# Routing among experts: a planner that counts VectorE's low parts from when they can begin, flag tiles cleared first, single tiles counted in round 0

## Chip, cores and metric

One core of a Trainium2 chip runs the kernel. The metric is the device time of one execution in microseconds (us), lower is better. The profiler's span (first to last instruction of the program) is a little shorter than the device time.

## What is computed

Attention over 4 x 8 heads of 768 tokens (a window of 31 keys around each query, and 24 block summaries), whose output of 3072 tokens x 512 goes into a mixture of 8 experts. The routing is greedy over all token-expert pairs in the order of their logits, with 384 places per expert:

```python
logits = x @ w_gate                       # 3072 x 8
for idx in np.argsort(-logits.flatten()):
    tok, e = idx // E, idx % E
    if assigned[tok] >= 0 or counts[e] >= cap:   # cap = 3072 // 8 = 384
        continue
    assigned[tok] = e; counts[e] += 1
for e in range(E):
    mask = assigned == e
    out[mask] = np.maximum(x[mask] @ w1[e], 0.0) @ w2[e]    # 512 -> 1024 -> 512
```

## The kernel before, in words

**Three parts follow each other.** Attention, ordered by a list scheduler of its own (`plan`), ends with the logits of 24 tiles of 128 tokens. Routing round 0 then finds the first expert that fills up, and its 384 tokens. Then eight experts run one after the other, in the order in which they fill; here they are called expert 0 to expert 7. Round r+1 of the routing runs beside expert r or earlier ones, piece by piece.

**An expert** has two stages on TensorE. The h stage is 96 matmuls of 128x384 (8 blocks f of 12, L786), the y stage 72 matmuls of 128x512 (24 groups of 3, L803). All products are made of a high and a low part: ScalarE copies a high part (`ah`, `bh` of the weights, `xh` of the tokens, `hh` of the hidden values), VectorE subtracts it and so leaves the low part (`al`, `bl` L620, `xl` L654, `hl` L793). The tokens of the next expert are gathered from DRAM (`xg`, GpSimd's queue) and transposed on TensorE into PSUM banks, 3 transposes for each of 4 slices of the model dimension; one such group of 3 is called a flip here (`flip_x`). The 4 PSUM banks of the flips are those in which the next h stage accumulates.

**A round of routing** is a serial chain between TensorE and VectorE. `aim` marks each token's best expert with places left. `search` then finds a rank threshold in 3 digits, and is done twice: for a digit, `compare` writes 0/1 tiles for 24 token tiles (VectorE, in two halves, `g`), 12 small matmuls count them per expert (L471, called a count here), VectorE turns the counts into flags (`full`, L475 to L477), a single matmul reduces the flags (L480, called a step), and VectorE sets the next thresholds (`piv`, L484). In a count one matmul takes two token tiles at once: tile t against its own experts and tile t+1 against its own, with 16 columns, of which two blocks are used and added. After the second search two prefix matmuls (L548, L549) and 12 matmuls (L580) give the 384 token indices; `close` and the next `aim` follow.

**The planner** is a clock in Python, not on the chip: `state["now"]` advances by a cost for each matmul that is written out (0.174 for the h stage, 0.228 for the y stage), and `state["dve"]` says until when VectorE has work. `service` writes out low parts that are due, and `advance` the next piece of the routing as soon as its wait has passed on that clock. So costs and waits in `TUNE` decide between which expert matmuls a routing matmul stands, and TensorE, ScalarE and VectorE each then work in the order written. `prepare` places the flips of the next expert in the y stage: from group 9 on if the round is finished and the tokens were fetched `xw` before, at intervals of `fp`; whatever is left stands behind the last y matmul.

```python
def vector(cost):                                        # L694
    state["dve"] = max(state["dve"], state["now"] + TUNE["hop"]) + TUNE["dv"] * cost
```

Round 0 is not among experts: nothing else is left for TensorE, and its steps follow each other as fast as they can. GpSimd has work of its own before the first flags: `count`, `place` and `slot` (L455 to L460), which use SBUF space that attention held until its last output tiles are in DRAM, and then the clearing of the two flag tiles `full0`, `full1` (L464).

## Time and profile before

| | before |
|---|---|
| device time, 3 runs | 488.83, 490.3, 491.13 us (median 490.3) |
| profiled execution | 490.43 us, of it span 488.7 us |
| attention | 0 to 135 us of the span |
| round 0 up to the first expert matmul | 135 to 164 us |
| eight experts | 164.3 to 479.3 us |
| last rows to DRAM | to 488.7 us |
| TensorE busy | 449.5 us (92%) |
| VectorE busy | 348.8 us (71%) |
| ScalarE, GpSimd busy | 212.7 us, 129.8 us |

The busy time of an engine is a mean over stages with different limits. A matmul's row shows when it starts and how long until its result is there; matmuls of one kind start closer to each other than their rows are long. "idle before" in square brackets is the time in which the engine had nothing to do before a row, and what released it.

### The profile page before, as it was taken

The page shows a single profiled execution, that of the slowest core. Times are in us where ns is not written, and L with a number is a line of the kernel's source. Part 1 is how long each engine was busy: PE and PEld are TensorE (multiplying, and loading weights), DVE is VectorE, ACT ScalarE, POOL GpSimd, SP SyncE. Part 2 cuts the span into 40 slices and gives each one's busy share as a digit, 9 for nine tenths or more (in the row PEclk, how much of TensorE's full clock was granted, in tenths as well). Part 3 has the DMA queues.
Part 4 walks back from the last instruction along what each step waited for, and adds up shares of the span by engine and source line. Part 5 has one row for each costly group of instructions (what it writes and reads, how often), then busy time and mean ns, then how long its engine had stood idle before and what let it go on. Part 6 is the DMA issues. An engine that isn't in the chain of part 4 may idle for free.

```text
span 488.7 us, 12165 instructions
## 1 busy us (share of the span) xinstructions
PE 449.5 (92%) x4655; PEld 374.2 (77%) x4655; DVE 348.8 (71%) x1349; ACT 212.7 (44%) x449; POOL 129.8 (27%) x211
## 2 busy tenths in 40 slices
PE   7999999999925899999989989999998998999992
PEld 6686877878814797698778779769877876989981
DVE  5989888869758888867777777786778756561510
ACT  3796877858401442441353154144125306443400
POOL 2596939234111101400320230040023025002010
PEclk9999999999955999999999999999999998999997
DMA  8998392211203803800930660380083069621001
GB/s 307 410 313 314 92 393 89 74 46 67 89 1 108 302 2 131 317 28 18 331 126 1 229 245 1 108 336 32 4 317 154 1 218 345 235 87 65 1 23 43
DMA packets 22426, 73.32 MB, mean 150 GB/s; under 512 B 3168, under 2 KB 3424, under 8 KB 21984
## 3 DMA queue, kind: packets, MB, share of 16 engines
q1 hardware_dynamic: 16608, 53.67, 30.6%
q0 software_dynamic: 5760, 18.88, 10.3%
q8 instruction: 37, 0.61, 0.5%
q14 instruction: 21, 0.17, 0.1%
HBM read 59.95 MB, written 12.58 MB: 148 GB/s over the span
## 4 chain that ended last, share of the span: by engine, by line
PE 70%; issue 13%; DVE 10%; DMA 3%; POOL 2%; ACT 1%; POOLq 0%; SPq 0%; DVEq 0%
PE h L786 21%; PE y L803 20%; PE o L366 6%; PE s L330 5%; PE t L134 5%; DVE al L620 4%; PE x L134 3%; PE l L372 3%; PE r L471 3%; DVE g L106 1%; POOL out L769 1%; DVE xl L654 1%; PE x L272 1%; PE y L739 1%; DMA xd<-x 1%
## 5 line engine op out<-in xcount | busy, mean ns | idle before, releaser
L803 PE MATMUL y<-bl,hh 128*128 128x512 f32 x192 | 76.9, 401 | 0.0
L803 PE MATMUL y<-bh,hl 128*128 128x512 f32 x192 | 76.8, 400 | 0.0
L803 PE MATMUL y<-bh,hh 128*128 128x512 f32 x192 | 76.5, 399 | 0.0
L631 POOL DMA_INDIRECT xg<-xd,idx x24 | 23.2, 968 | 188.4 <-issue 136.8
L617 ACT ACTIVATE ah<-raw 128x1024 fp32r<-128x1024 f32 (+1 forms) x36 | 34.0, 965 | 83.6 <-DMA raw<-w1r 65.6
L786 PE MATMUL h<-xh,ah 128*128 128x384 f32 x256 | 60.4, 350 | 8.1 <-DVE xl L654 3.6
L790 ACT ACTIVATE hh<-h 128x384 fp32r<-128x384 f32 x64 | 31.5, 491 | 83.0 <-PE h L786 70.0
L786 PE MATMUL h<-xl,ah 128*128 128x384 f32 x256 | 61.1, 347 | 0.7
L793 DVE SCALAR_TENSOR_TENSOR hl<-h,hh 128x384 fp32r<-128x384 f32 x64 | 35.4, 553 | 35.2 <-ACT hh L790 32.6
L345 ACT ACTIVATE pe<-sm,mx 128x120 f32<-128x120 f32 x192 | 57.8, 385 | 0.3
L786 PE MATMUL h<-xh,al 128*128 128x384 f32 x256 | 56.4, 341 | 0.0
L769 POOL DMA_INDIRECT out<-y,idx x24 | 29.6, 1233 | 98.8 <-ACT y L767 92.4
L786 PEld LDWEIGHTS h<-xh,ah 128*128 128x128 f32 x256 | 45.2, 191 | 12.6 <-ACT xh L651 5.7
L786 PEld LDWEIGHTS h<-xl,ah 128*128 128x128 f32 x256 | 45.4, 189 | 3.7 <-DVE xl L654 3.7
L786 PEld LDWEIGHTS h<-xh,al 128*128 128x128 f32 x256 | 45.6, 190 | 0.0
L338 DVE CUSTOM_DVE_ANT_0 sm<-s,cs 128x120 f32<-128x120 f32 x192 | 41.2, 277 | 5.5 <-PE s L330 4.9
L803 PEld LDWEIGHTS y<-bh,hh 128*128 128x128 f32 x192 | 36.1, 188 | 6.5
L803 PEld LDWEIGHTS y<-bh,hl 128*128 128x128 f32 x192 | 36.2, 189 | 6.2
L803 PEld LDWEIGHTS y<-bl,hh 128*128 128x128 f32 x192 | 36.2, 188 | 6.1
L620 DVE TENSOR_TENSOR al<-raw,ah 128x1024 fp32r<-128x1024 f32 (+1 forms) x36 | 38.9, 1097 | 0.6 <-ACT ah L617 0.6
L620 DVE TENSOR_TENSOR bl<-raw,bh 128x1024 fp32r<-128x1024 f32 x32 | 38.9, 1215 | 0.0
L617 ACT ACTIVATE bh<-raw 128x1024 fp32r<-128x1024 f32 x32 | 33.7, 1053 | 1.0 <-DMA raw<-w2r 1.0
(139 smaller groups left out, 738.1 us busy)
## 6 DMA issues: line engine op xcount, KB each, us to landing
raw<-w1r SPq DMA_DIRECT2D x32, 512.0 KB
raw<-w2r SPq DMA_DIRECT2D x32, 512.0 KB, 4.2
kd<-kT SPq DMA_DIRECT2D x16, 400.0 KB, 5.5
vw<-v SPq DMA_DIRECT2D x24, 260.0 KB, 10.1
xd<-x POOLq DMA_DIRECT2D x24, 256.0 KB
qt<-qT SPq DMA_DIRECT2D x3, 1536.0 KB
qt<-qT SPq DMA_DIRECT2D x3, 512.0 KB
xg<-xd,idx POOLq DMA_INDIRECT x24
```

The source lines that it names most:

```text
L134: nc.tensor.transpose(o, i, idn)
L330: nc.tensor.matmul(PS[2 * t + k][x * 64:x * 64 + 64, p], QT[b % 2][r, (i + x) // FIRST, p, (i + x) % FIRST], keys(b, p, r, i + x), start=T ...
L338: nc.vector.tensor_tensor_reduce(sm[:, p], PS[u][:, p], m, -0.125, 3e38, op0=OP.add, op1=OP.min, accum_out=mx[:, p:p + 1])
L345: nc.scalar.activation(PE_[u][:, p], SM[u][0][:, p], AF.Exp, bias=SM[u][1][:, p:p + 1], scale=-1.0)
L366: nc.tensor.matmul(po(t, s)[x * 64:x * 64 + 64, p], PT[u][:, p, x * 64:x * 64 + 64], VW[b % 2][:C, i - s + x, 2 * p + s], start=True, stop ...
L617: nc.scalar.activation(hi[:, c], raw[:, c], AF.Copy)
L620: nc.vector.tensor_tensor(lo[:, c], raw[:, c], hi[:, c].bitcast(F32), op=OP.subtract)
L769: st = nc.gpsimd.indirect_dma_start(out=out, out_offset=bass.IndirectOffsetOnAxis(ap=ROUND[r][1][:, c:c + 1], axis=0), in_=y, in_offset=None)
L786: nc.tensor.matmul(ph, a[:, d], b[:, d], start=n == 0, stop=n == 11)
L790: nc.scalar.activation(hh[:, f], ph, AF.Relu)
L793: nc.vector.scalar_tensor_tensor(hl[:, f], ph, 0.0, hh[:, f].bitcast(F32), op0=OP.max, op1=OP.subtract)
L803: nc.tensor.matmul(py[c], a[:, f, s], b, start=f == 0 and i == 0, stop=f == 7 and i == 2)
```

## The change

Four things. The planner's `vector` takes a time since which the work can begin, and low parts pass the time at which their high part was written out plus `lb` (0.75) or `wb` (1.25), instead of the time at which they themselves are written out. The waits of the routing pieces have other numbers and a second part that occupies VectorE without delaying the next matmul; a flip costs 0.57 on the planner's clock instead of 0.33, a count 0.36 instead of 0.41. The two flag tiles are cleared near the program's start. In round 0 a count takes single token tiles: 24 matmuls of 8 columns, and one instruction on VectorE makes the flags and their maximum. Rounds 1 to 7 keep pairs.

```diff
-    y2=0.45, y2m=0.021, y3=1.7,
+    y2=0.55, y2m=0.0064, y2r=0.23, y3=1.25, y3r=0.5, lb=0.75, wb=1.25, fx=0.57,
...
+    fulls = [rt.tile([128, E + 1], BF, name=f"full{k}") for k in range(2)]
+    for full in fulls:
+        nc.gpsimd.memset(full, 0.0)
+
     first = targets(0)
...
-    fulls = [rt.tile([128, E + 1], BF, name=f"full{k}") for k in range(2)]
-    for full in fulls:
-        nc.gpsimd.memset(full, 0.0)
-
-    def search(R, oh, dup, g, digits):
+    def search(R, oh, dup, g, digits, pairs):
         for i, n in enumerate(digits):
-            pc = R[:, 384:384 + 2 * E]
-            for t in range(0, NT, 2):
-                nc.tensor.matmul(pc, g[t // HT][:, t % HT * n:t % HT * n + 128], oh[:, t:t + 2].rearrange("p t e -> p (t e)"), start=t == 0, stop=t == NT - 2)
+            m = 2 if pairs else 1
+            pc = R[:, 384:384 + m * E]
+            for t in range(0, NT, m):
+                nc.tensor.matmul(pc, g[t // HT][:, t % HT * n:t % HT * n + 128], oh[:, t:t + m].rearrange("p t e -> p (t e)"), start=t == 0, stop=t == NT - m)
...
-            nc.vector.tensor_scalar(short[:n], pc[n:2 * n, E:], -1.0, CAP - 0.5, op0=OP.mult, op1=OP.add)
-            nc.vector.tensor_tensor(full[:n, :E], pc[:n, :E], short[:n], op=OP.is_ge)
-            nc.vector.tensor_reduce(full[:n, E:], full[:n, :E], axis=AX.X, op=OP.max)
-            yield 0.017 * NT, TUNE["y1"]
+            if pairs:
+                short = rt.tile([64, E], F32, name="short", bufs=2)
+                nc.vector.tensor_scalar(short[:n], pc[n:2 * n, E:], -1.0, CAP - 0.5, op0=OP.mult, op1=OP.add)
+                nc.vector.tensor_tensor(full[:n, :E], pc[:n, :E], short[:n], op=OP.is_ge)
+                nc.vector.tensor_reduce(full[:n, E:], full[:n, :E], axis=AX.X, op=OP.max)
+            else:
+                nc.vector.tensor_scalar(full[:, :E], pc, CAP - 0.5, 0.0, op0=OP.is_ge, op1=OP.max, accum_out=full[:, E:])
+            yield 0.36, TUNE["y1"]
...
-                yield 0.03, TUNE["y2"] + m * TUNE["y2m"]
+                yield 0.05, TUNE["y2"] + n * TUNE["y2m"], TUNE["y2r"] + n * TUNE["y2m"]
...
-            yield 0.03, TUNE["y3"]
+            yield 0.05, TUNE["y3"], TUNE["y3r"]
...
-            def low(c=c):
+            def low(c=c, since=state["now"] + TUNE["wb"]):
                 nc.vector.tensor_tensor(lo[:, c], raw[:, c], hi[:, c].bitcast(F32), op=OP.subtract)
-                vector(0.06 + 1.08 / n)
+                vector(0.06 + 1.08 / n, since)
...
-    def vector(cost):
-        state["dve"] = max(state["dve"], state["now"] + TUNE["hop"]) + TUNE["dv"] * cost
+    def vector(cost, since=None):
+        state["dve"] = max(state["dve"], state["now"] + TUNE["hop"] if since is None else since) + TUNE["dv"] * cost
...
-            state["now"] += 0.33
+            state["now"] += TUNE["fx"]
```

What this does to the order is seen in three places. Up to the end of attention all engines keep their order, but for two clears on GpSimd.

The first place is GpSimd's queue ahead of round 0. Before:

```order
L455 TENSOR_SCALAR count<-colsi 128x128 x3
L457 CAST place<-cb 128x2
L459 TENSOR_TENSOR slot<-cb 128x3
L460 TENSOR_SCALAR slot<-slot 128x3
L464 MEMSET full_2940 128x9
L464 MEMSET full_2941 128x9
```

And of the change, GpSimd's first rows in the program, ahead of all work that waits for a transfer:

```order
L96 MEMSET g_77 128x832
L96 MEMSET g_78 128x832
L96 MEMSET g_79 128x832
L96 MEMSET g_80 128x832
L138 MEMSET full_85 128x9
L138 MEMSET full_86 128x9
```

The clears no longer stand behind `count`.

The second place is TensorE at the end of expert 2's y stage, where expert 3's tokens are flipped (`h<-cs,xg`), a step stands (`r<-full,steps`) and expert 3's first matmuls follow. Before:

```order
L134 MATMUL h<-cs,xg 128x128 x3
L803 MATMUL y<-bl,hh 128x512
L480 LDWEIGHTS steps
L480 MATMUL r<-full_2941,steps 128x9
L803 MATMUL y<-bh,hl 128x512
L803 MATMUL y<-bh,hh 128x512
L803 MATMUL y<-bl,hh 128x512
L803 MATMUL y<-bh,hl 128x512
L803 MATMUL y<-bh,hh 128x512
L134 MATMUL h<-cs,xg 128x128 x9
L786 MATMUL h<-xh,ah 128x384 x4
```

Of the change, the end of the same stage, with the first matmuls of a count behind the last y matmul:

```order
L807 MATMUL y<-bl,hh 128x512
L484 LDWEIGHTS steps
L484 MATMUL r<-full_86,steps 128x9
L807 MATMUL y<-bh,hl 128x512
L807 MATMUL y<-bh,hh 128x512
L807 MATMUL y<-bl,hh 128x512
L807 MATMUL y<-bh,hl 128x512
L807 MATMUL y<-bh,hh 128x512
L472 LDWEIGHTS g_77
L472 MATMUL r<-oh,g_77 128x16
```

No flip is left there; the four stand behind y matmuls 30, 39, 48 and 57 of the 72. Expert by expert, the y matmuls behind which the next expert's four flips stand are: before 66, 72, 72, 72 in experts 0 to 4, then 63, 69, 72, 72 in expert 5 and 27, 39, 51, 63 in expert 6; of the change 60, 66, 72, 72 in expert 0, then 54, 66, 69, 72 in expert 1, then 30, 39, 48, 57 in experts 2 to 4, and 27, 36, 45, 54 in experts 5 and 6. The rounds run ahead: the routing's last matmul before stands behind y matmul 66 of expert 5, and of the change behind h matmul 29 of that expert.

The third place is VectorE at the same end of expert 2's y stage. Before, up to expert 3's first count:

```order
L106 TENSOR_TENSOR g_78<-dup,piv 128x768
L488 TENSOR_SCALAR below<-piv 128x1
L620 TENSOR_TENSOR al<-raw,ah 128x1024
L654 TENSOR_TENSOR xl<-h,xh 128x384
L620 TENSOR_TENSOR al<-raw,ah 128x1024
L654 TENSOR_TENSOR xl<-h,xh 128x384
L620 TENSOR_TENSOR al<-raw,ah 128x1024
L654 TENSOR_TENSOR xl<-h,xh 128x384 x2
L475 TENSOR_SCALAR short<-r 64x8
```

Of the change, from the last `xl` of that stage on:

```order
L658 TENSOR_TENSOR xl<-h,xh 128x384
L477 TENSOR_SCALAR short<-r 32x8
L478 TENSOR_TENSOR full_86<-r,short 32x8
L479 TENSOR_REDUCE full_86<-full_86 32x1
L488 TENSOR_SCALAR piv<-cs,r 128x32
L106 TENSOR_TENSOR g_77<-dup,piv 128x384
L106 TENSOR_TENSOR g_78<-dup,piv 128x384
L492 TENSOR_SCALAR below<-piv 128x1
L477 TENSOR_SCALAR short<-r 32x8
```

The three `al` and four `xl` that stood last have moved forward in the stage, and search steps stand at its end.

## Rows read from the trace of the kernel before

**Rows 1.** The page's first lines: the span, and TensorE's busy time, share of the span and instructions.

```profile
span 488.7 us, 12165 instructions
...
PE 449.5 (92%) x4655; PEld 374.2 (77%) x4655; DVE 348.8 (71%) x1349; ACT 212.7 (44%) x449; POOL 129.8 (27%) x211
```

**Rows 2.** Busy time of each engine by stage, cut at the first matmul of each h and y stage: h and y of expert 0, 1, 4, 5 and 6, and h of expert 7. Behind the colon of a stretch stands its length, then the engines as the first line names them.

```profile
core 0: us, PE busy (x) PEld busy (x) DVE busy (x) ACT busy (x) POOL busy (x), PEclk, DMA share, GB/s
...
164.30:183.35 19.05, 19.05 (x149) 17.79 (x150) 16.28 (x44) 9.42 (x15) 0.00 (x0) 1.00 0.33 129
183.35:204.54 21.19, 20.30 (x139) 15.49 (x138) 16.71 (x65) 5.94 (x9) 4.94 (x8) 1.00 0.59 210
204.54:224.27 19.73, 19.41 (x136) 17.44 (x136) 14.95 (x36) 8.90 (x15) 2.09 (x3) 1.00 0.18 70
224.27:245.48 21.21, 20.30 (x138) 15.46 (x137) 16.46 (x64) 5.99 (x9) 5.00 (x8) 1.00 0.62 223
...
327.41:347.19 19.78, 19.45 (x135) 17.48 (x136) 14.95 (x36) 8.85 (x15) 2.15 (x3) 1.00 0.15 59
347.19:368.36 21.17, 20.28 (x139) 15.47 (x138) 16.47 (x64) 5.99 (x9) 5.02 (x8) 1.00 0.60 213
368.36:388.10 19.74, 19.40 (x136) 17.44 (x137) 14.96 (x36) 8.85 (x15) 2.16 (x3) 1.00 0.17 66
388.10:408.27 20.17, 19.66 (x120) 14.97 (x120) 13.85 (x57) 4.55 (x8) 3.97 (x6) 1.00 0.60 214
408.27:428.70 20.43, 18.80 (x99) 18.11 (x98) 11.29 (x16) 10.28 (x16) 6.90 (x10) 0.92 0.74 270
428.70:446.53 17.83, 17.83 (x86) 14.65 (x85) 8.55 (x10) 7.33 (x11) 0.29 (x1) 1.00 0.15 54
446.53:463.19 16.66, 16.66 (x97) 16.66 (x96) 7.30 (x10) 7.96 (x13) 2.93 (x6) 1.00 0.13 48
```

**Rows 3.** The timeline where round 0's first flags are made: start, length, engine, line, operation.

```profile
135.64 0.17 DVE L475 TENSOR_SCALAR short<-r 64x8 f32<-64x8 f32 x1 [0.33 <-PE r L471]
135.88 1.54 POOL L455 TENSOR_SCALAR count<-colsi 128x128 f16<-128x128 int16 x3 [3.98 <-DMA xd<-x]
...
137.96 0.15 POOL L464 MEMSET full<- 128x9 bf16 x2
138.10 0.16 DVE L476 TENSOR_TENSOR full<-r,short 64x8 bf16<-64x8 f32 x1 [2.30 <-POOL full L464]
...
138.51 0.19 PE L480 MATMUL r<-full,steps 128*128 128x9 bf16 x1 [2.98 <-DVE full L477]
```

**Rows 4.** Later steps of round 0 in the timeline, and, as the last line, a group of the list by line: the accumulator reads that follow attention's masked minimum (shapes, count, busy us and mean ns).

```profile
140.06 0.16 DVE L475 TENSOR_SCALAR short<-r 32x8 f32<-32x8 f32 x1 [0.36 <-PE r L471]
140.33 0.15 DVE L476 TENSOR_TENSOR full<-r,short 32x8 bf16<-32x8 f32 x1
140.51 0.15 DVE L477 TENSOR_REDUCE full<-full 32x1 bf16<-32x8 bf16 x1
...
140.72 0.19 PE L480 MATMUL r<-full,steps 128*128 128x9 bf16 x1 [0.70 <-DVE full L477]
...
144.73 0.47 PE L471 MATMUL r<-oh,g 128*128 128x16 bf16 x12 [1.64 <-DVE wh L516]
...
L338 DVE DVE_READ_ACCUMULATOR2_ANT mx<- 128x1 f32 x192 | 15.9, 83 | 0.0
```

**Rows 5.** The timeline where expert 2 hands over to expert 3.

```profile
282.55 0.49 PE L134 MATMUL h<-cs,xg 128*128 128x128 f32 x3
...
284.41 1.15 PE L134 MATMUL h<-cs,xg 128*128 128x128 f32 x9
...
286.31 1.21 DVE L620 TENSOR_TENSOR al<-raw,ah 128x1024 fp32r<-128x1024 f32 x1
286.45 0.62 PE L786 MATMUL h<-xh,ah 128*128 128x384 f32 x2 [0.89 <-DVE xl L654]
```

**Rows 6.** The timeline of a count and of a step among y matmuls of expert 2.

```profile
281.01 0.46 PE L471 MATMUL r<-oh,g 128*128 128x16 bf16 x12
281.33 0.47 PE L803 MATMUL y<-bh,hl 128*128 128x512 f32 x1
281.64 0.39 PE L803 MATMUL y<-bh,hh 128*128 128x512 f32 x1
...
283.12 0.18 PE L480 MATMUL r<-full,steps 128*128 128x9 bf16 x1
283.15 0.48 PE L803 MATMUL y<-bh,hl 128*128 128x512 f32 x1
```

**Rows 7.** The end of a round among experts, from the prefix matmul on, in the timeline; then two groups of the page, with shapes, count, busy us and mean ns.

```profile
271.37 0.18 PE L548 MATMUL r<-inc,cb 128*128 128x2 bf16 x1
...
271.61 0.41 DVE L555 SCALAR_TENSOR_TENSOR place<-inc,r,ge 128x24 f16<-128x24 bf16 x2 [0.63 <-PE r L549]
...
273.84 0.16 DVE L581 COPY hit<-r 128x3 f32<-128x3 f32 x1
...
277.73 0.36 DVE L127 TENSOR_TENSOR oh<-cand,tgt 128x192 bf16<-128x192 bf16 x1
...
L793 DVE SCALAR_TENSOR_TENSOR hl<-h,hh 128x384 fp32r<-128x384 f32 x64 | 35.4, 553 | 35.2 <-ACT hh L790 32.6
L620 DVE TENSOR_TENSOR bl<-raw,bh 128x1024 fp32r<-128x1024 f32 x32 | 38.9, 1215 | 0.0
```

More of the change, by code (lines that the diff above doesn't have):

```diff
@@ L481, in search @@
             if i < 2:
-                m = digits[i + 1]
+                n = digits[i + 1]
                 piv = rt.tile([128, 64], I16, name="piv", bufs=2)
-                nc.vector.tensor_scalar(piv[:, :m], offs[:, FROM[digits][i]:FROM[digits][i] + m], ps[:, E:], below, op0=OP.add, op1=OP.add)
+                nc.vector.tensor_scalar(piv[:, :n], offs[:, FROM[digits][i]:FROM[digits][i] + n], ps[:, E:], below, op0=OP.add, op1=OP.add)
                 g = steps_tile()
-                compare(g, dup, piv, m)
+                compare(g, dup, piv, n)
                 below = rt.tile([128, 1], F32, name="below", bufs=2)
                 nc.vector.tensor_scalar(below, piv[:, :1], -STEPS[STEP[digits][i + 1]][0], None, op0=OP.add)
-                yield 0.03, TUNE["y2"] + m * TUNE["y2m"]
+                yield 0.05, TUNE["y2"] + n * TUNE["y2m"], TUNE["y2r"] + n * TUNE["y2m"]
         return (below, ps[:, E:]), ps[:, :E], ps[:, E:]
@@ L506, in route @@
         if r < E - 1:
-            at, won, top = yield from search(R, oh, T["dup"], T["g"], T["digits"])
+            at, won, top = yield from search(R, oh, T["dup"], T["g"], T["digits"], r > 0)
             d = rt.tile([128, NT], F32, name="d", bufs=2)
@@ L516, in route @@
             nc.vector.scalar_tensor_tensor(wh, won, top, w8f, op0=OP.is_equal, op1=OP.mult)
-            yield 0.03, TUNE["y3"]
-            at, won, top = yield from search(R, oh, dup2, g, EVEN)
+            yield 0.05, TUNE["y3"], TUNE["y3r"]
+            at, won, top = yield from search(R, oh, dup2, g, EVEN, r > 0)
             wl = rt.tile([128, E], F32, name="wl", bufs=2)
@@ L651, in split_x, with low @@
         nc.scalar.activation(xh[:, d], p, AF.Copy)
-        def low():
+        def low(since=state["now"] + TUNE["lb"]):
             nc.vector.tensor_tensor(xl[:, d], p, xh[:, d].bitcast(F32), op=OP.subtract)
-            vector(0.55)
+            vector(0.55, since)
         later.append((state["now"] + TUNE["xlo"], low))
@@ L790, in expert, with low @@
             nc.scalar.activation(hh[:, f], ph, AF.Relu)
-            def low(f=f, ph=ph):
+            def low(f=f, ph=ph, since=state["now"] + TUNE["lb"]):
                 nc.vector.scalar_tensor_tensor(hl[:, f], ph, 0.0, hh[:, f].bitcast(F32), op0=OP.max, op1=OP.subtract)
-                vector(0.55)
+                vector(0.55, since)
             later.append((state["now"] + TUNE["lo"], low))
```

5 lines of the change are left out of this document (2 added, 3 removed).

## The prediction, made before the result

> **What bounds the kernel now.** I read the page's first lines first: TensorE is busy for 92% of the span [rows 1], so a gain must come from its idle time or from work taken off it. Next the busy time by stage, cut at the first matmul of each h and y stage. Two stages carry no routing and no late flip: y of expert 6 (17.83 us) and h of expert 7 (16.66 us) [rows 2]. Together 34.5 us is what an expert costs TensorE if nothing is waited for. The reader should compare experts 1 to 4 with that: 40.94 us each (19.73 + 21.21 in the first, 19.78 + 21.17 in the last of the four) [rows 2]. Part of the difference is the routing's own matmuls. A count takes 0.32 us until the next y matmul, and that one another 0.08 more than the usual 0.23 (0.31), so 0.40; a step 0.03 and as much behind it, 0.12 [rows 6]. Six counts, six steps, one prefix pair (like a step, 0.14) and 12 index matmuls (like a count, 0.40) make 3.66 us a round. 34.5 + 3.66 = 38.15, so each of these experts loses 2.8 us to waits.
>
> Where, the timeline of a hand-over shows: nine of the twelve flip matmuls start at 284.41, behind the last y matmul; at 0.11 us each they are issued by 285.4, and expert 3's first matmul starts at 286.45, released by the `xl` of a flip, while an `al` has begun at 286.31 and more `al` and `xl` stand behind it [rows 5]. Late flips meet late weight splits on VectorE. It is not that VectorE has no time: it is busy 16.46 of 21.21 us in the y stage and 14.95 of 19.73 in the h stage [rows 2].
>
> The other losses by the same arithmetic: expert 0 40.24 us with four counts and steps in h (2.1) and the rest in y (2.1), 1.5 lost; expert 5 39.91 with three counts and steps, one prefix pair and six index matmuls (2.0), 3.4; expert 6 38.26 without routing, 3.8. With 4 x 2.8 that is 19.9 us in all.
>
> Round 0 lies outside: a serial chain in which every microsecond counts. Its first flags could be made at 135.8; VectorE instead idles 2.30 us until GpSimd has cleared the flag tile, which stands behind `count`, which waited 3.98 us for the output tiles of attention [rows 3].
>
> **The change part by part.** All sums are made against the profiled execution, 490.43 us, which lies 0.13 above the median of the three.
>
> *Clearing first.* The clears move to GpSimd's start, ahead of its first wait for a transfer. The 2.30 us go [rows 3]. `count` itself, done by 137.4, is next needed by the spans at the end of round 0, some 15 us later. **-2.3.**
>
> *Single tiles in round 0.* Six counts get 12 matmuls more. Twelve take 0.47 us of which 0.17 is the last one's own latency, so 0.027 each [rows 4]: 0.32 more where both halves of the thresholds are there, about half where TensorE would have waited for the second half anyway, and 0.03 in the first count, which runs ahead tile by tile. I take 1.0 for the six (0.8 to 1.6). On VectorE three instructions become one. They run from 140.06 to 140.66, and the step starts at 140.72 [rows 4]. The trace has no compare that also writes a maximum. Below, it costs like the first of the three, 0.16; above, 0.16 and an accumulator read of 0.083, as behind attention's masked minimum [rows 4], with 0.04 between, 0.28. I take 0.28, since that is the nearest instruction with such an output. This saves 0.6 - 0.34 = 0.26 a step, 1.6 in six (at best 2.3). [...] **-0.6** (-1.5 to 0).
>
> *Flips and splits earlier.* The planner now believes VectorE free sooner, places routing steps sooner, and each round gains on the experts until, from expert 2 on, a round is done before the y stage in which its tokens are flipped begins or early in it. Then four flips stand at y matmuls 30, 39, 48 and 57, 15 matmuls (3.5 us) before the stage ends, as expert 6 had it before without a wait. So the hand-overs from experts 2 to 6 become free. That from expert 0 does not: two flips still stand last, and behind them ScalarE has an output copy, a split of `ah` and two copies `xh`, about 2.8 us; less the flips and three matmuls, 1.6 us stay. From expert 1 one flip stands last: 0.2. Expert 0 keeps 0.4 in its h stage.
>
> *New waits.* A routing matmul placed earlier waits if VectorE is late, and all of TensorE's expert matmuls queue behind it. I went through each pair in the new order: the distance on TensorE (0.174 us an h matmul, 0.23 a y matmul, the blocks above) against the chain on VectorE. Most have room. The tight ones: in expert 0 a step stands one flip and one y matmul behind its count, 0.95 us, where count to step took 1.2 in round 0 even at once: 0.3, and the next count 0.3; expert 1 two counts behind an `al`, 0.5; expert 2 a step with one flip and four y matmuls before the count of the second search, 1.4 against 1.8: 0.4. In expert 3 the end of a round shows the mechanism best. Between prefix pair and next count stand 51 h matmuls and the 12 index matmuls, 51 x 0.174 + 0.54 = 9.4 us. VectorE needs 0.24 to `place`, 2.23 until `hit`, 4.25 from there to the end of `oh` [rows 7], and in the new order two `bl` and two `hl` stand between, 2 x 1.21 + 2 x 0.55 [rows 7]: 10.2. So 0.8. About nine steps that follow their count at once cost 0.1 each. All told 3.3. These are counted one by one, while one late step makes the next late and a low part in front of a step can itself wait for ScalarE. I take 6; below 3, above 13, which is what six rounds with 11 handovers each would lose at 0.2 apiece.
>
> Experts: 19.9 before, afterwards 0.4 + 1.6 + 0.2 + 6 = 8.2. **-11.7** (-14.7 to -4.7).
>
> Sum: 490.4 - 2.3 - 0.6 - 11.7 = **475.8 us**.
>
> **Rivals.** (1) *Waits take half back.* New waits are 13 us rather than 6: 483. For it: the planner charges an end of round less than the 6.7 us of VectorE rows above, and it no longer has the slack that late low parts gave it. Against: my pairs show room nearly everywhere. [...] (3) *The change doesn't do what it says.* Not the flips but `al` on VectorE holds the next h stage [rows 5], and in the new order, with search steps at the end of the stage, VectorE is as late as before: only clearing, single tiles and expert 6's loss remain, 490.4 - 2.9 - 3.8 = 484. Against: the `al` move forward too. (4) *Slower.* In VectorE's queue at the end of a round low parts stand ahead of the rank work; if each of five rounds waits there, it decides from 14.6 / 5 = 2.9 us a round, which is a `bl` and an `hl` more than once over what I count (0.8 in the worst). At 3.4 a round: 493.
>
> **How the numbers follow.** Forecast 0.66, rival 1 0.17, rival 2 0.07, rival 3 0.05, rival 4 0.05. The forecast's own bounds are 490.4 - 2.3 - 1.5 - 14.7 = 472 and, with 8 us of new waits, 478; the range takes in rivals 1 and 2: **471 to 483.5 us**. Half a percent, 2.5 us, is about what this kernel's runs (488.83 to 491.13) can tell from no change. Rivals 1 to 3 are all faster by more, but rival 3 could lose its remainder: faster 0.91, same 0.04, slower 0.05.
>
> **What would show it.** In the trace of the change: no idle before the first flags of round 0 and about 2.9 us less from attention's end to expert 0; one VectorE instruction and a read of 0.08 between count and step. h of experts 3 and 4 near 19 us, y of experts 2 to 4 between 20 and 21, h of expert 6 16.7 at clock 1.00; no wait of an h matmul for `xl` or `xh` from expert 3 on; 1 to 2 us left at the start of expert 1. [...] The prediction fails above all if VectorE's queue makes the search steps later than the pairs say.

## The result: 477.65 us, and the profile after

The changed kernel takes 477.65 us (median; 476.95 to 478.95) against 490.14 for the kernel before on the same chip: ratio 0.975, 95% interval 0.9718 to 0.9782. Timed a second time beside the experiments it took 475.98 us, ratio 0.9741 (0.9713 to 0.9769). The forecast was 475.8 in a range of 471 to 483.5, so the size was right. Its parts were not all right, and that is what the experiments are about.

The first profiled execution of the changed kernel (477.92 us). The page's first lines, against [rows 1]:

```profile
span 476.2 us, 12327 instructions
...
PE 444.8 (93%) x4727; PEld 374.8 (79%) x4727; DVE 345.4 (73%) x1343; ACT 214.5 (45%) x449; POOL 128.2 (27%) x211
```

TensorE's busy time fell by 4.7 us although it issues 72 matmuls more; the other 7.8 us of the 12.5 by which the span shrank are idle time. Three stretches add up to it: from attention's last `oh` (its end) to the first expert matmul 28.98 us before and 25.63 now; from there to the last y matmul's start 315.04 and 305.3; the tail 9.3 in both; attention's end itself came 0.6 later.

Stages of the changed kernel, cut as in [rows 2], from its second profile (why the second, the next section tells): h and y of experts 0, 1 and 4, then y of expert 5 and h of expert 6. Behind the colon of a stretch stands its length; the last number but two is the granted clock.

```profile
161.21:180.25 19.04, 19.04 (x149) 17.78 (x150) 16.27 (x44) 9.42 (x15) 0.00 (x0) 1.00 0.32 126
180.25:202.03 21.78, 20.71 (x150) 15.64 (x150) 17.46 (x68) 5.16 (x8) 3.99 (x6) 1.00 0.63 221
202.03:222.23 20.20, 19.24 (x140) 17.45 (x139) 15.85 (x40) 9.66 (x16) 3.31 (x5) 1.00 0.13 50
222.23:242.42 20.19, 20.15 (x139) 15.48 (x138) 17.38 (x65) 6.72 (x10) 3.74 (x6) 1.00 0.71 247
...
322.80:341.67 18.87, 18.87 (x149) 17.73 (x147) 17.23 (x60) 7.84 (x13) 6.98 (x10) 1.00 0.75 256
341.67:361.68 20.01, 20.01 (x139) 15.40 (x139) 18.16 (x61) 7.28 (x11) 0.24 (x1) 1.00 0.38 139
...
378.80:396.62 17.82, 17.82 (x85) 14.66 (x85) 8.55 (x10) 7.27 (x11) 0.23 (x1) 1.00 0.51 173
396.62:413.29 16.67, 16.67 (x98) 16.66 (x96) 7.30 (x10) 8.01 (x13) 6.28 (x10) 1.00 0.54 163
```

Expert 0 gained nothing (40.82 us against 40.24), expert 1 half a microsecond, expert 4 two, and from y of expert 5 on every stage has the length of a stage without waits. The gain grows from expert to expert, because each round of routing is done a little earlier than the one before it. From the same profile, TensorE's waits after its first expert matmul by what ended them (total us, times, longest):

```profile
PE h L134 <- DMA xg<-xd,idx: 1.1, 2, 0.8
PE h L790 <- DVE xl L761: 0.9, 1, 0.9
PE h L790 <- ACT xh L655: 0.9, 1, 0.9
PE r L472 <- DVE wh L520: 0.3, 1, 0.3
PE r L472 <- DVE below L492: 0.2, 1, 0.2
```

Waits of a routing matmul (the last two) come to half a microsecond in this list, which leaves short waits out. The rest of the list is at the start of expert 0 (`xl`, 0.9, as before), at expert 0's flips, which wait for the gather of the tokens (1.1), and at the hand-over from expert 0 to 1 (`xh`, 0.9). The hand-over from expert 2 to 3, where [rows 5] showed nine flip matmuls and a wait for `xl`, is now a count and the first h matmuls right behind it (timeline of the first profile):

```profile
283.57 0.46 PE L472 MATMUL r<-oh,g 128*128 128x16 bf16 x12
...
283.89 0.96 PE L790 MATMUL h<-xh,ah 128*128 128x384 f32 x4
```

Round 0, where [rows 3, 4] had three VectorE instructions for a flag tile and an idle time of 2.30 us (timeline of the first profile):

```profile
136.26 0.17 DVE L481 TENSOR_SCALAR_CACHE_REDUCE full<-r 128x8 bf16<-128x8 f32 x1 [0.38 <-PE r L472]
136.35 0.09 DVE L481 DVE_READ_ACCUMULATOR full<-r 128x1 bf16 x1
...
137.40 0.80 PE L472 MATMUL r<-oh,g 128*128 128x8 bf16 x24 [0.73 <-DVE g L106]
...
138.24 0.17 DVE L481 TENSOR_SCALAR_CACHE_REDUCE full<-r 128x8 bf16<-128x8 f32 x1 [0.56 <-PE r L472]
138.33 0.09 DVE L481 DVE_READ_ACCUMULATOR full<-r 128x1 bf16 x1
...
138.47 0.17 PE L484 MATMUL r<-full,steps 128*128 128x9 bf16 x1 [0.27 <-DVE full L481]
```

The first flags wait for their count only (0.38). From the first flag instruction to the step are 0.23 us, 0.66 before [rows 4]; from the start of a count to its flags 0.84, where 12 matmuls took 0.63. A step gains 0.2.

### The profile page after: what moved, and what is told of

It reads as the page before. It is cut to its first block, busy times and chain, and to the rows that moved or that the text cites. A ratio compares the mean times of both kernels' runs of the same rounds, so it can differ in the third digit from the quotient of the medians.

```text
span 476.2 us, 12327 instructions
## 1 busy us (share of the span) xinstructions
PE 444.8 (93%) x4727; PEld 374.8 (79%) x4727; DVE 345.4 (73%) x1343; ACT 214.5 (45%) x449; POOL 128.2 (27%) x211
## 4 chain that ended last, share of the span: by engine, by line
PE 46%; issue 14%; DVE 2%; POOL 1%; DMA 1%; ACT 1%; POOLq 0%; ACTq 0%
PE y L807 21%; PE h L790 21%; PE r L472 2%; PE h L134 2%; POOL out L773 1%; DMA xg<-xd,idx 1%; DVE g L106 1%; ACT ah L621 0%; PE r L584 0%; ACT y L771 0%; POOL xg L635 0%; DVE al L624 0%; POOLq L883 0%; ACT xh L655 0%; PE r L484 0%
## 5 line engine op out<-in xcount | busy, mean ns | idle before, releaser
L807 PE MATMUL y<-bl,hh 128*128 128x512 f32 x192 | 78.3, 408 | 0.0
L773 POOL DMA_INDIRECT out<-y,idx x24 | 25.8, 1073 | 171.0 <-ACT y L771 164.4
L790 PE MATMUL h<-xh,ah 128*128 128x384 f32 x256 | 58.2, 343 | 1.9 <-DVE xl L761 1.0
L790 PE MATMUL h<-xl,ah 128*128 128x384 f32 x256 | 58.3, 342 | 0.0
L621 ACT ACTIVATE ah<-raw 128x1024 fp32r<-128x1024 f32 (+1 forms) x36 | 32.7, 957 | 38.3 <-DMA raw<-w1r 29.2
L655 ACT ACTIVATE xh<-h 128x384 fp32r<-128x384 f32 x28 | 13.8, 493 | 63.8 <-PE h L134 63.7
```

The costliest lines, as they stand in the source:

```text
L621: nc.scalar.activation(hi[:, c], raw[:, c], AF.Copy)
L655: nc.scalar.activation(xh[:, d], p, AF.Copy)
L773: st = nc.gpsimd.indirect_dma_start(out=out, out_offset=bass.IndirectOffsetOnAxis(ap=ROUND[r][1][:, c:c + 1], axis=0), in_=y, in_offset=None)
L790: nc.tensor.matmul(ph, a[:, d], b[:, d], start=n == 0, stop=n == 11)
L807: nc.tensor.matmul(py[c], a[:, f, s], b, start=f == 0 and i == 0, stop=f == 7 and i == 2)
```

## The experiments

Every kernel was timed beside the kernel before on the same chip; ratios are to that.

| kernel | us | ratio | 95% interval |
|---|---|---|---|
| changed, first time | 477.65 | 0.975 | 0.9718 to 0.9782 |
| clearing put back | 476.53 | 0.9729 | 0.97 to 0.9759 |
| pairs in round 0 | 476.19 | 0.971 | 0.9686 to 0.9733 |
| planner of before | 485.95 | 0.9941 | 0.9916 to 0.9966 |
| bookkeeping alone | 476.74 | 0.9739 | 0.9697 to 0.9781 |
| before, again | 490.02 | 1.0001 | 0.997 to 1.0031 |
| changed, again | 475.98 | 0.9741 | 0.9713 to 0.9769 |
| numbers alone | 477.17 | 0.9753 | 0.9727 to 0.9779 |
| flips last | 477.79 | 0.9771 | 0.9743 to 0.9799 |
| splits late | 480.67 | 0.983 | 0.9796 to 0.9864 |
| both late | 489.91 | 1.0 | 0.9977 to 1.0023 |
| gather first | 475.3 | 0.9707 | 0.9681 to 0.9732 |
| optimist | 498.65 | 1.0193 | 1.0161 to 1.0226 |

### Round 0: the clearing and the pairs

Clearing put back behind `count`:

```diff
-    fulls = [rt.tile([128, E + 1], BF, name=f"full{k}") for k in range(2)]
-    for full in fulls:
-        nc.gpsimd.memset(full, 0.0)
-
     first = targets(0)
...
+    fulls = [rt.tile([128, E + 1], BF, name=f"full{k}") for k in range(2)]
+    for full in fulls:
+        nc.gpsimd.memset(full, 0.0)
+
     def search(R, oh, dup, g, digits, pairs):
```

> The changed kernel with the clearing of the two flag tiles put back behind `count` on GpSimd; all else as changed, and the order of every instruction among the experts is the same. By the prediction the clearing is worth the 2.30 us that VectorE idled before the first flags [rows 3]: 477.65 + 2.3 = 480.0 us, and in the trace the first flag instruction idles about 2.3 us behind GpSimd's clearing, with from attention's last `oh` to the first expert matmul 25.6 + 2.3 = 27.9 us. A rival: the whole 3.35 us by which that stretch became shorter are the clearing's, and single tiles gave nothing: 481.0. A second: another wait stands behind the first, and putting the clearing back costs nothing: 477.7. Beside it, since the order among the experts is that of the changed kernel: in the trace of the changed kernel `hit` of expert 4's h stage starts 1.8 us behind the index matmul it reads (0.22 elsewhere, where VectorE is free), and the next count waits 1.47 us. If that belongs to the order, it shows again here; if it belongs to that one execution, `hit` follows in 0.25 us and the count waits for nothing.

Pairs in round 0:

```diff
-            at, won, top = yield from search(R, oh, T["dup"], T["g"], T["digits"], r > 0)
+            at, won, top = yield from search(R, oh, T["dup"], T["g"], T["digits"], True)
...
-            at, won, top = yield from search(R, oh, dup2, g, EVEN, r > 0)
+            at, won, top = yield from search(R, oh, dup2, g, EVEN, True)
```

> The changed kernel, but round 0 counts pairs of tiles as before; the order among the experts is unchanged. By the prediction single tiles are worth 0.6 us (0 to 1.5): 478.25. By the step rows of the two traces, where six intervals from step to step became shorter by 0.04 to 0.29 us each, 1.1 us: 478.75, with about 1.1 us more between attention's last `oh` and the first expert matmul. If the first flags also gained only through the clearing, nothing: 477.65. The same second look at `hit` in expert 4 as in the run with the late clearing: 1.8 us behind its matmul if the order makes it so, 0.25 if not.

By time neither can be told from the changed kernel; the three intervals overlap. The traces tell them apart. The measure is round 0's chain, from the start of attention's last `oh` to the start of the first gather of tokens on GpSimd. In the changed kernel (first profile):

```profile
135.66 0.22 DVE L127 TENSOR_TENSOR oh<-cand,tgt 128x16 bf16<-128x16 bf16 x1
...
153.03 1.06 POOL L635 DMA_INDIRECT xg<-xd,idx  x1 [16.33 <-DVE pos L568]
```

That is 17.37 us. The same two rows with the clearing put back, and with pairs:

```profile
136.10 0.17 DVE L127 TENSOR_TENSOR oh<-cand,tgt 128x16 bf16<-128x16 bf16 x1
...
153.97 1.06 POOL L635 DMA_INDIRECT xg<-xd,idx  x1 [16.82 <-DVE pos L568]
```

```profile
135.61 0.22 DVE L127 TENSOR_TENSOR oh<-cand,tgt 128x16 bf16<-128x16 bf16 x1
...
154.01 1.06 POOL L635 DMA_INDIRECT xg<-xd,idx  x1 [17.36 <-DVE pos L568]
```

That is 17.87 us and 18.40: the clearing is worth 0.50 and single tiles 1.03. Together 1.53, yet the kernel before took 20.71, 3.34 more. So the kernel before was profiled again, unchanged.

> The kernel before, unchanged, profiled a second time. In the five profiles taken since (the change and four runs of parts) GpSimd waits 2.35 to 2.40 us for the output tiles of attention ahead of `count`, in the profile of before it waited 3.98 [rows 3]; and with the clearing alone put back, VectorE idles 0.86 us before the first flags, not 2.30. If the 3.98 belong to that one execution, this profile shows about 2.4, an idle of about 0.9 before the flags, and from attention's last `oh` to the first expert matmul 25.6 + 0.95 (pairs) + 0.45 (clearing) = 27.0 us instead of 28.98. If they belong to the kernel before, 3.98, 2.30 and 29.0 again. The fall of the granted clock in h of expert 6 [rows 2] likewise: with the same order among the experts the run with the planner of before shows that stage at 1.00 and 19.08 us; if the fall is a chance of single executions, it need not come here either. Time 490 either way.

Its rows for `count`, the second clearing and the first flags, and the ends of the same chain:

```profile
134.36 1.58 POOL L455 TENSOR_SCALAR count<-colsi 128x128 f16<-128x128 int16 x3 [2.36 <-DMA xd<-x]
...
135.51 0.22 DVE L127 TENSOR_TENSOR oh<-cand,tgt 128x16 bf16<-128x16 bf16 x1
...
136.49 0.15 POOL L464 MEMSET full<- 128x9 bf16 x2
...
136.63 0.16 DVE L476 TENSOR_TENSOR full<-r,short 64x8 bf16<-64x8 f32 x1 [0.40 <-POOL full L464]
...
154.38 1.06 POOL L631 DMA_INDIRECT xg<-xd,idx  x1 [17.74 <-DVE pos L564]
```

The wait for attention's output tiles is 2.36 us here, not 3.98, the flags idle 0.40 us for the clearing, not 2.30 [rows 3], and the chain is 18.87 us: 1.50 above the changed kernel, the 0.50 and 1.03 of the two single runs. (The stretch to the first expert matmul was 28.52, not the 27.0 expected: behind the chain TensorE's matmuls stayed slow until 162.2. Between the flips of expert 0 eight warm-up matmuls (`warm`, whose results nobody reads) took 1.01 us at 159.82 and 0.96 at 161.49, against 0.61 at 162.73. In the first profiles of before and of the changed kernel the granted clock rose from 0.50 to 1.00 at 159.5 and at 155.0.) So 1.8 us of the 3.34 belong to one execution, in which the tiles landed late. That is no rarity: over the 14 profiles of this study GpSimd waited 2.35 to 2.40 us in eight and 3.46 to 4.17 in six. In the run with the flips last it was 3.57, and the clearing, now done long before, no longer lets that reach VectorE:

```profile
136.17 1.69 POOL L459 TENSOR_SCALAR count<-colsi 128x128 f16<-128x128 int16 x3 [3.57 <-DMA xd<-x]
136.39 0.17 DVE L481 TENSOR_SCALAR_CACHE_REDUCE full<-r 128x8 bf16<-128x8 f32 x1 [0.39 <-PE r L472]
```

In all ten profiles with the changed round 0 the chain is 17.3 to 17.4 us, five of them with late tiles; in the two of before it is 18.87 with early tiles and 20.71 with late ones. So the clearing first is worth 0.5 us with early tiles (eight profiles of fourteen) and some 2.3 with late ones.

### The changed kernel again

> The changed kernel, unchanged, profiled a second time and timed beside the others. If the late TensorE signals in h of experts 4 and 5 belong to the first profile's execution, `hit` follows its index matmul in 0.25 us there, the count of expert 4 waits for nothing, its h stage lasts 18.8 us as in the two runs with the same order, and the experts together about 303 us (305.3 in the first profile). If they belong to this kernel, 20.4 us and 305 again. Time: 477.65 by the first runs; by the two runs that undo a part of round 0 and came out no slower (476.5 and 476.2), it should then be 475.2 to 476.0.

In the first profile expert 4 had a wait of 1.47 us that no pair of the prediction explained. Its rows: the index matmuls, `hit` that reads them, ScalarE's `hh` of the same h block, and the count:

```profile
325.83 0.47 PE L584 MATMUL r<-place,span 128*128 128x25 f16 x12
...
327.92 0.16 DVE L585 COPY hit<-r 128x3 f32<-128x3 f32 x1 [1.57 <-PE h L790]
327.96 0.49 ACT L794 ACTIVATE hh<-h 128x384 fp32r<-128x384 f32 x1 [3.05 <-PE h L790]
...
332.23 0.46 PE L472 MATMUL r<-oh,g 128*128 128x16 bf16 x12 [1.47 <-DVE oh L127]
```

Two engines stand still until 327.9 for matmuls that were over by 326.8 (the profile models a matmul's end, but the next matmuls started in step: groups of four at 326.58, 327.30 and 328.00). The second profile, same program and same place:

```profile
324.56 0.47 PE L584 MATMUL r<-place,span 128*128 128x25 f16 x12
325.06 0.16 DVE L585 COPY hit<-r 128x3 f32<-128x3 f32 x1
...
329.37 0.46 PE L472 MATMUL r<-oh,g 128*128 128x16 bf16 x12
```

No delay, no wait, h of expert 4 is 18.87 us instead of 20.46, and the experts take 302.7 us instead of 305.3. The two runs on round 0, with the same order among the experts, show 303.1 and 302.7 and no delay either. So the wait belongs to one execution, in which `hh` and `hit` started 1.2 and 1.6 us behind the end of the matmuls that they read, for a reason that stays open. The second profile stands for the kernel from here on.

### Which edit of the planner carries the gain

The planner of before on the changed round 0 (the order among the experts is then that of before, instruction for instruction):

```diff
-    hop=0.22, dv=1.0, e5=2, e50=0, warm2=3.6192, adv=14, y0=2.6, y1=0.5, y2=0.55,
-    y2m=0.0064, y2r=0.23, y3=1.25, y3r=0.5, lb=0.75, wb=1.25, fx=0.57, y4=1.5,
+    hop=0.22, dv=1.0, e5=2, e50=0, warm2=3.6192, adv=14, y0=2.6, y1=0.5, y2=0.45,
+    y2m=0.021, y2r=0.0, y3=1.7, y3r=0.0, lb=0.75, wb=1.25, fx=0.33, y4=1.5,
...
-            yield 0.36, TUNE["y1"]
+            yield 0.017 * NT, TUNE["y1"]
...
-                yield 0.05, TUNE["y2"] + n * TUNE["y2m"], TUNE["y2r"] + n * TUNE["y2m"]
+                yield 0.03, TUNE["y2"] + n * TUNE["y2m"]
...
-            yield 0.05, TUNE["y3"], TUNE["y3r"]
+            yield 0.03, TUNE["y3"]
...
     def vector(cost, since=None):
+        since = None
```

> The changed kernel with the planner of before: its numbers, its costs of a count and a step, and low parts charged from the planned moment of writing; so the experts' instructions stand in exactly the order of before, and only the clearing and the single tiles of round 0 remain of the change. By the prediction 490.1 - 2.9 = 487.2 us; by the two traces (3.35 us less between attention's end and the first expert matmul) 486.8. The stages of experts 1 to 4 as before, near 19.7 and 21.2 us, and an expert 6 whose h stage starts with a wait and lasts over 19 us. If the earlier start of the experts let transfers or splits come in time by themselves, the experts would gain as well and the time fall below 485; if the gain ahead of the experts is eaten by their first waits, it stays near 490.

The ratio 0.9941 is 2.9 us, 1.7 to 4.1: round 0 is worth that by time, and the rest, some 10 us, is the planner's. The experts took 312.7 us in this profile, without the fall of the clock that cost expert 6 of before 1.35 us (h took 20.43 at a granted clock of 0.92 against 19.08 at 1.00).

Two runs take this edit apart. The bookkeeping alone is the same diff without its last line, so that `since` counts and the numbers are the old ones. The numbers alone is that last line by itself:

```diff
     def vector(cost, since=None):
+        since = None
```

> As the run with the planner of before, but low parts are charged to VectorE from when they can begin (0.75 and 1.25 us behind the planning of their copies): the bookkeeping alone, with the numbers and costs of before. In this order the routing gains on the experts slowly: the last flips stand at y matmul 72, 72, 69, 66 and 60 in experts 1 to 5, where before they stood three at 72. If flips that stand last are what costs an expert its 2.8 us, then experts 0 to 2 keep their hand-over waits, the others lose them, and expert 6 loses its 3.8: of the 9.7 us some 6, so 487 - 6 = 481. If the bookkeeping is the whole of the planner's gain, 477.7; if the numbers are, 487.

> The changed kernel without the new bookkeeping: low parts are charged to VectorE from the planned moment of writing again, but the new numbers and the costs of a count, a step and a flip stay. In its order the flips stand within three y matmuls of those of the change in every expert, and most routing matmuls at the same places. If the places of flips and routing set the time, it is that of the change: 477, within 1.5. If the bookkeeping itself carries the gain, as the few words on the change have it, 485 or more.

Either alone gives all of it, as far as the time can tell: 0.9739 and 0.9753 against 0.9741, with intervals of some 1.3 to 2 us to either side. My 481 for the bookkeeping was wrong. Its late flips of experts 0 to 2 cost as they did before (1.1 and 1.3 us of waits at the hand-overs into experts 1 and 2 are in its trace), but rounds that gain a little on each expert free the later ones, and expert 0, whose order it leaves as it was, loses less than in the changed kernel (40.1 against 40.8 us). So the title's planner "that counts VectorE's low parts from when they can begin" names one sufficient cause, not the necessary one: what both edits do is let the planner place a round's steps sooner, so that the round takes less of an expert.

### Flips and splits, early and late

Three runs and the changed kernel make a table of two by two: the flips of an expert's tokens early or at the end of the y stage, the splits of its `a` weights (`ah` on ScalarE, `al` on VectorE) early or at the end.

Flips last:

```diff
-    ap=1.6, qf=8.3981, xw=5.4012,
+    ap=1.6, qf=23.5, xw=5.4012,
```

Splits late:

```diff
-        if q and p["a"] < 4 and p["w"] is not None and now >= p["last"] and (q > TUNE["ql"] or now >= p["w"] + TUNE["aw"] + TUNE["as_"] * p["a"]):
+        if q and p["a"] < 4 and p["w"] is not None and q >= (18, 21, 23, 24)[p["a"]]:
```

Both late is this second edit and

```diff
-        elif q > TUNE["qf"] and p["d"] < 4 and p["x"] is not None and (q > TUNE["ql"] or now >= max(p["x"] + TUNE["xw"], p["flip"])):
+        elif q >= (22, 24, 24, 24, 25)[p["d"]] and p["d"] < 4 and p["x"] is not None and (q > TUNE["ql"] or now >= max(p["x"] + TUNE["xw"], p["flip"])):
```

> The changed kernel, but all four flips of an expert wait for the last y matmul (the planner's earliest group for a flip is 23.5 instead of 8.4); the new bookkeeping, numbers and round 0 stay, and the routing steps keep going early. This takes the early flips alone away. By the prediction late flips are what the planner's part is about (of 19.9 us lost before, 3.8 at expert 6 and near 2 at the others at the hand-over): with all four last each hand-over costs at least what it cost before (1.1 to 1.6 us of waits before the first h matmuls), now at every one of seven, experts 5 and 6 too: 7 x 2.0 - 0.9 that the change has = +13, about 490. If instead the earlier search steps carry the gain and the hand-over is covered by other work, 478 to 480.

> The changed kernel, but the four splits of `ah` of the next expert are planned at y matmuls 54, 63, 69 and 72, where they stood before; the flips keep their early places (from expert 3 on 27 to 57). Together with the run with the flips last and the next one this is a table of two by two: flips early or late, splits early or late. My theory after the run with late flips (only 0.2 us of wait at most hand-overs where before they cost 2.7): neither alone is dear; what costs is flips AND splits late, because `xl` and `xh` then queue behind `al` and `ah` on VectorE and ScalarE. With the flips early the last two `al` are needed only at h matmuls 49 and 73, 8 us into the stage: so no wait at the start of h, about 476 + 0.5. The rival, rival 3 of the prediction (`al` on VectorE holds the next h stage whatever the flips do): 2 us at each of seven hand-overs, 488 to 490.

> The changed kernel with both late: splits of `ah` at y matmuls 54, 63, 69 and 72, flips at 66 and three at 72, as before in experts 0 to 4; new bookkeeping, numbers and round 0 stay. If late flips behind late splits are the whole of what the planner's part gained, each of seven hand-overs costs the 2.7 us that it cost before (y to h, and the first twelve h matmuls), against 3.4 at the first, 0.9 at the second and nothing at the others in the changed kernel: 7 x 2.7 - 4.3 = +14.6, near 490. If late flips and late splits only add up, from the run with late flips +1.8 and nothing or little for the splits: 478.

I had expected 490 from late flips alone. They cost little: 0.9771 against 0.9741 is 1.5 us, and the two intervals overlap. Both late gave 489.9, the whole gain gone, with the new bookkeeping and round 0 still in. Its experts took 317.8 us in its profile, 2.8 more than those of before: the hand-over into expert 7, free before, is late here too, and the granted clock was 0.93 over h of expert 2. The cleanest place is the hand-over from expert 6 to 7, where no routing is left: y of expert 6 and h of expert 7 in the changed kernel, with flips last, with splits late, and with both late.

```profile
413.29:431.12 17.83, 17.83 (x86) 14.65 (x86) 8.55 (x10) 7.28 (x11) 0.24 (x1) 1.00 0.16 54
431.12:447.78 16.66, 16.66 (x97) 16.66 (x96) 7.30 (x10) 8.00 (x13) 2.96 (x6) 1.00 0.13 48
```

```profile
415.27:433.30 18.03, 17.84 (x86) 14.70 (x85) 6.84 (x8) 6.62 (x11) 1.69 (x3) 1.00 0.18 61
433.30:450.09 16.79, 16.79 (x97) 16.70 (x98) 8.64 (x13) 8.24 (x14) 1.53 (x4) 1.00 0.11 40
```

```profile
417.90:435.73 17.83, 17.83 (x86) 14.65 (x85) 6.37 (x8) 5.46 (x9) 0.23 (x1) 1.00 0.16 57
435.73:452.40 16.67, 16.67 (x98) 16.67 (x97) 9.66 (x12) 9.54 (x15) 3.50 (x6) 1.00 0.13 49
```

```profile
428.01:445.64 17.63, 17.63 (x86) 14.67 (x85) 4.65 (x6) 4.47 (x7) 0.83 (x1) 1.00 0.16 53
445.64:464.48 18.84, 17.56 (x99) 16.77 (x98) 11.01 (x15) 10.15 (x17) 2.75 (x6) 1.00 0.11 43
```

The sums are 34.49, 34.82, 34.50 and 36.47 us: late flips cost 0.33, late splits nothing, both 1.98. Late flips are dear only behind late splits. The other hand-overs of the run with the flips last agree: 0.2 us of waits into experts 4 to 6, where all splits are long done, but 1.2 and 1.6 into experts 1 and 2, where an `al` stands between the `xl` or just ahead of them. Why, the timeline of that hand-over shows with both late:

```profile
445.64 0.42 PE L790 MATMUL h<-xh,ah 128*128 128x384 f32 x1
...
445.84 1.07 ACT L621 ACTIVATE ah<-raw 128x1024 fp32r<-128x1024 f32 x1
...
446.79 1.26 ACT L655 ACTIVATE xh<-h 128x384 fp32r<-128x384 f32 x3
446.94 1.23 DVE L624 TENSOR_TENSOR al<-raw,ah 128x1024 fp32r<-128x1024 f32 x1 [0.21 <-ACT ah L621]
447.34 1.21 PE L790 MATMUL h<-xh,ah 128*128 128x384 f32 x3 [1.28 <-ACT xh L655]
```

The `ah` that TensorE needs last (this `ah` is the last quarter, used from h matmul 73 on) stands ahead of the `xh` that it needs at once, and `al` ahead of `xl` on VectorE. Both engines' rows here start in the order written: the last flips are over by 445.89, but the first `xh` starts at 446.79, behind the `ah` of 1.07 us that began at 445.84, and the next `xl` at 448.08, behind the `al` of 1.23 us that began at 446.94.

Splits late came out at 480.7, not at 476.5, and its own trace says where most of it is: its rounds were slower, so that the tokens of experts 1 to 3 still had a flip at y matmul 72, behind late splits. Into experts 1, 2 and 3 `xh` kept TensorE waiting 1.0, 1.0 and 1.5 us, where the changed kernel waits 0.9 once; the experts took 307.5 us, 4.8 more. Why the rounds were slower is not shown. Into experts 4 to 7, whose flips stood at 27 to 57, nothing waited, though an `ah` and two `al` stood last.

### Two more

> The changed kernel with expert 1's first flip held 0.5 us longer by the planner, so that it stands at y matmul 63 of expert 0 rather than at 60, where TensorE waited 0.84, 1.42, 0.60 and 1.07 us for the gather of the tokens in the four profiles with that order. A later flip also comes nearer to the hand-over. If the gather wait is a pure loss: y of expert 0 21.8 - 1.1 = 20.7 us, the experts together 301.6 rather than 302.7, the time 475. If the wait only moves to the hand-over (flips at 63, 69 and 72): no change, 476.

```diff
-        elif q > TUNE["qf"] and p["d"] < 4 and p["x"] is not None and (q > TUNE["ql"] or now >= max(p["x"] + TUNE["xw"], p["flip"])):
+        elif q > TUNE["qf"] and p["d"] < 4 and p["x"] is not None and (q > TUNE["ql"] or now >= max(p["x"] + TUNE["xw"] + (0.5 if r == 1 else 0.0), p["flip"])):
```

The wait was neither removed nor moved. With the flip three y matmuls later TensorE still waited 1.28 us for the gather; in that execution it landed later (the flip matmul that waits last for it starts at 198.18, against 197.63 in the second profile of the changed kernel). y of expert 0 stayed at 21.8 us and the experts at 303.2. By time, 475.3 us at 0.9707 (0.9681 to 0.9732), it cannot be told from the changed kernel. No run beat the changed kernel by more than the measurement can tell.

> The changed kernel with every cost that the planner charges to VectorE taken at three quarters (`dv` 0.75 instead of 1.0). It places the routing steps still earlier: all rounds are done in expert 3, and the flips of experts 1 to 6 stand at y matmuls 27 to 58. This tests rival 1 of the prediction: routing matmuls placed before VectorE is ready hold up the expert matmuls behind them. In the changed kernel the waits on counts, steps and index matmuls are only 0.6 us in all, so its numbers are above VectorE's times somewhere. If they are above by a quarter, no new waits, and the hand-overs from experts 0 and 1 become free too: 476 - 3.5 = 472.5. If they are right or nearly so, each of six rounds (each some 17 us of charged VectorE time) waits up to 4 us: 476 - 3.5 + 6 x 2 = 484 (up to 496).

```diff
-    hop=0.22, dv=1.0,
+    hop=0.22, dv=0.75,
```

498.65 us, slower than before (1.0161 to 1.0226). The hand-overs are free, and TensorE waits for VectorE instead; the same view as above, its first three lines:

```profile
PE r L472 <- DVE oh L127: 8.9, 5, 2.5
PE r L484 <- DVE full L479: 2.6, 6, 0.9
PE r L472 <- DVE wh L520: 2.3, 5, 0.8
```

The experts took 325.1 us, 22.4 more than the changed kernel. The longest wait for `oh` was 2.5 us, and the mean granted clock of the execution 0.963, against 0.971 in the second profile of the changed kernel. The changed numbers thus stand close to the edge: at 1.0 waits of routing matmuls come to half a microsecond in that list, at 0.75 to 16.6.

## Why the prediction was right, point by point

**What bounds the kernel.** Right, and shown by the run with both late: late flips behind late weight splits [rows 5] are enough to take the whole gain back. That this lands at the very time of before is partly chance, since one more hand-over is late there and round 0 is shorter. And "late flips" was too short a name, and I used it that way when I expected 490 from late flips alone.

**Clearing first, -2.3.** Mis-sized. The step that failed is "The 2.30 us go": it took the row of one execution for the usual one. Measured 0.5 with tiles that land early, and about 2.3 only where they land late, as in [rows 3].

**Single tiles, -0.6.** Measured -1.0, with both terms off in opposite directions. Flags to step came to 0.23 us and not 0.34 (0.28 and 0.06 to the step), since the accumulator read follows 0.09 behind the start of the first instruction: 0.43 saved a step, 2.6 in six. The twelve matmuls more cost 0.21 at the place shown and about 1.5 in six by the difference, where I took 1.0.

Together round 0 came to -1.5 in the chain instead of -2.9, -3.3 against the profiled execution of before, and -2.9 (1.7 to 4.1) by time in the run with the planner of before. An estimate from the chains, 1.5 and with late tiles in six profiles of fourteen another 1.8, is 2.3 in the mean, which that interval holds as well.

**Experts, -11.7.** Measured 315.04 to 302.70, -12.3. The arithmetic of the prediction, an expert free of waits at 34.5 us and the routing blocks at their prices, applied to the second profile (experts 0 to 5 now hold 8, 6, 8, 7, 6 and 0 counts, 7, 7, 7, 8, 6 and 0 steps, one prefix pair each and two in expert 3, and 12 index matmuls each, 24 in expert 4 and 6 in expert 5):

| us lost in expert | 0 | 1 | 2 | 3 | 4 | 5 | 6 | sum |
|---|---|---|---|---|---|---|---|---|
| before, as predicted from | 1.5 | 2.8 | 2.8 | 2.8 | 2.8 | 3.4 | 3.8 | 19.9 |
| changed, measured | 1.7 | 2.1 | 1.3 | 1.0 | 0.3 | 0.1 | 0.0 | 6.5 |

The first line should sum to 18.9: in expert 5 of before there are 48 count matmuls, 4 steps, 2 prefix pairs and 18 index matmuls, 3.0 us and not the 2.0 that I counted, so that it lost 2.4. The forecast for the second line was 8.2, as 0.4 + 1.6 + 0.2 + 6. So the losses before were taken 1.0 too high and those after 1.7 too high, and the two nearly cancel: that the gain came out within 0.6 us of the forecast is in part luck.

The mis-sized term is the new waits, 6. The list above has 0.5 us of them. With the short waits that it leaves out it is more: by the starts of TensorE's matmuls in the second profile, the 34 counts that stand by themselves held the next expert matmul up by 1.8 us beyond their 0.32 each, the 35 of before by 0.8. Even the 3.3 counted pair by pair were too many. The end of a round in expert 3, forecast to wait 0.8, waited some 0.2: from the first prefix matmul (289.94 in the first profile) to the end of `oh` (299.53) 9.6 us passed, not the 10.2 of the sum, which set rows end to end that overlap on VectorE (a `bl` of 1.22 us starts at 292.41, the row behind it at 293.55). Nor had I a term for the gather: expert 0's flips moved ahead of the landing of their tokens (0.6 to 1.4 us in the profiles with that order). The waits of the list are 3.4 of the 6.5 us; the rest has not been taken apart in full.

**Rivals.** Rival 1 (new waits of 13 us) did not happen here, but it is real: at three quarters of the charged times it costs more than the whole gain. Rival 2, with a chance of 0.07 in the forecast, was a fall of the granted clock in an expert stage. In both profiles of the changed kernel the expert stages are at 1.00, so it did not happen here either. The clock did fall in the run with both late (0.93 over h of expert 2). In the two profiles of before it fell in different stages: to 0.92 in h of expert 6 [rows 2], and in the second profile in h of expert 1:

```profile
204.37:225.02 20.65, 20.42 (x135) 18.95 (x136) 14.95 (x36) 8.90 (x15) 2.11 (x3) 0.92 0.18 68
```

There it cost 0.9 us (20.65 against 19.73 in the first profile), in h of expert 6 the 1.35 above. Rival 3 (`al` holds the h stage whatever the flips do) is refuted by the run with late splits, in experts 4 to 7. Rival 4 (low parts ahead of the rank work, from 2.9 us a round) fell with the end of expert 3's round.

**What would show it.** h of experts 3 and 4 near 19 (19.2 and 18.9), y of experts 2 to 4 between 20 and 21 (20.8, 20.8, 20.0), h of expert 6 at 16.7 and clock 1.00, no h matmul that waits for `xl` or `xh` from expert 3 on, 1 to 2 us left at the start of expert 1, one VectorE instruction and a read of 0.09: all as said. The wait of 1.47 us before a count, of the kind that rivals 1 and 4 mean, belonged to one execution.

## To carry to other kernels

In this kernel, two engines that prepare the next stage in order cost little where only one kind of their work was late (0.33 us and nothing at the hand-over from expert 6 to 7, against 1.98 with both); look for the place where both are, since there what is needed last stands ahead of what is needed first. A planner that charged a shared engine too much held its own steps back, and one that charged a quarter too little stalled the bound engine: move such numbers in small steps and read both kinds of wait. Before a wait of the profile becomes a term of a sum, profile the same kernel a second time: here 1.6 us of one row and 1.5 of another were gone.

## What the runs showed of the hardware

The store of attention's last output tile (256 KB) took one of two lengths of time in the same code: GpSimd's wait behind it was 2.35 to 2.40 us in eight profiles and 3.46 to 4.17 in six. In the first profile of before, one of the six, it landed 4.23 us after its issue; in the first of the changed kernel, one of the eight, `count` started 2.92 us after that issue. What decides it was not tried.

In the first profile of the changed kernel VectorE and ScalarE went on late behind matmuls that were over: by up to 1.6 us in expert 4 and up to 2.8 in expert 5 (`hit` at 372.85, its index matmuls over by 370.1), while TensorE's matmuls went on at their pace (groups of four h matmuls at 371.26, 371.95 and 372.64). In the second profile they did not: `hit` of expert 4 starts at 325.06, its index matmuls over by 325.03. What delayed the two engines was not tried.

A wait of the same length came with a fall of the granted clock and without one. In the first profile of before TensorE stood still for 1.63 us ahead of the third h matmul of expert 6 (at 410.50), and the granted clock of that stage was 0.92. In the second profile of before it stood still for 1.64 us between 407.00 and 412.07, at the same hand-over, and the clock was 1.00 there and over the 19.08 us that follow; the run with the planner of before has that stage at 1.00 too. What decides whether the clock falls was not tried.
